# Early preparation of four head pairs and denser routing steps in a top-k attention and expert kernel

## The chip, the core and the metric

The kernel runs on one core of one Trainium2 chip. Five engines work from queues of their own: PE (matmuls and transposes), DVE (VectorE), ACT (ScalarE), POOL (GpSimd) and SP, which here issues nearly all DMAs. The metric is the device time of one execution in microseconds, median of several runs.

## The reference

Two layers are computed. The first is attention over q, k and v of 8 batches, 8 heads, 576 rows and 64 columns, in which each row keeps only its 32 largest scores. The second sends each of the 4608 output rows (512 wide) to one of 8 experts.

```
scores = (q @ k^T) / sqrt(64)
kth    = 32nd largest of each row
attn   = softmax over the scores >= kth
x      = attn @ v, heads side by side           # 4608 x 512
logits = x @ w_gate + modality_bias[modality]
e, p   = argmax and its softmax probability     # per row
out    = p * (relu(x @ w1[e]) @ w2[e])          # w1 512x1024, w2 1024x512
```

## The kernel before

Heads are taken in pairs, 32 pairs p from 0 to 31, four to a batch. A pair has 9 row tiles of 128 rows, so there are 288 tiles. One loop runs over steps i, with p = i // 9 and j = i % 9. A step works on several tiles at once: PE multiplies the scores of tile i+2 (L396), ACT copies them to SBUF (`Ssb`, L404), DVE takes the 8 largest of seven slices of tile i (seven MAX8, L411), merges those of tile i-1 (a chain of five, L422 to L424), ACT counts by a sign (`K`, L443) for tile i-3, POOL multiplies `y = Ssb * K` (L449) for tile i-4, DVE searches `y` of tile i-5 (L453), picks the threshold every third step (`eq`, `jk`, L460 to L462), ACT takes the exponential (`ex`, L467) of tile i-6, and DVE keeps the chosen ones of tile i-7 (`P`, L473). A one-element POOL instruction that reads `P` (`gate`, L477) holds POOL until that is done; `y` follows it.

Ahead of a pair its keys and queries must be turned and split. In steps j = 0, 1, 3 of pair p, `prep` turns tails, k and q of pair p+1 on PE; ACT writes a rounded part to the tile `st` (L275), PE subtracts it, and one step later ACT writes the rest (L279). Then `stack` issues DMAs that copy `st` to `ks` (six, L316) and `qs` (four, L318) in the layout of the matmul. There is one buffer for `st`.

When a batch's 36 steps are through, its 576 rows are routed: logits, argmax, ranks within experts (`route`), about 20 small DVE instructions, then five indirect DMAs from POOL (`send`, L620) that put the rows into lists per expert in DRAM (`xs`). Routing instructions lie in a queue `side`, slot choices in `rush`; each step takes up to SN = 4 of the one or RN = 6 of the other, and puts them among the seven MAX8 by holding up to four of these back (HOLD). For batches below EB = 3 (`early`) rows are turned in five steps running, and a send is issued behind `y`; for later ones the sends go through `side`, ahead of the step's gate and `y`.

Experts are worked in slots of 256 rows. `more_moe` starts a slot when its rows are counted (`seen`), and a budget (`spare_pe`, 3.3 a step less the listed costs) says how many matmuls of the slot a step takes. Twelve slots run inside the loop, in plain float32; those left run behind the loop in a three-term split form (`slot`). Until the first slot PE runs six filler matmuls a step (`keep_warm`, L931).

Of the kernel before, what the change touches and what calls it, by code (L numbers as in the profile page):

```python
# [9 lines left out]
FT = mybir.dt.float32  # L10
FR = mybir.dt.float32r
# [15 lines left out]
SN = 4  # L27
# [5 lines left out]
LJ = (5, 6)  # L33
# [2 lines left out]
QL = 2  # L36
HOLD = 4
NDIR = 2
KL = 2
LY = KL + 2  # L40
LT = LY + 1
# [9 lines left out]
PB = 6  # L51
COST = {"trans": 0.5, "qk": 0.5, "mix": 1.12, "rest": 0.22, "t": 0.11, "prep": 0.43, "logits": 1.2, "xrow": 0.54, "av": 0.42, "av8": 0.17}
RN = 6
QO = 0
EB = 3
RLF = (0, 1)
RXF = (3, 4, 5, 6, 7)
RLM = (3, 4)
# [12 lines left out]
def kernel(  # L71
# [43 lines left out]
    PAUSE = lambda: None  # L115
    WAIT = lambda: None

    def load(p, what, b=None, queues=(SP, SP, SP)):

        o = LD.setdefault(p, {})  # L120
        h0 = 2 * (p % HP)
        for nm in what:
            src = {"k": k, "q": q, "v": v}[nm]
            g = src[p // HP] if b is None else src[ds(b, 1)].rearrange("o h s d -> (o h) s d")
            if nm == "k":
                o["kq"] = ld.tile([128, 2, D], FT, name="kqt", bufs=1)
            t = vtb[p % 2] if nm == "v" else o["kq"][:64] if nm == "k" else o["kq"][64:]
            m = ld.tile([128, 2, 4, D] if nm == "v" else [128, 4, 2, D], FT, name=nm + "m", bufs=2 if nm == "v" else 1)
            if nm == "v":
                SP.dma_start(m.rearrange("p h c d -> p h (c d)"),  # L130
                             g[h0:h0 + 2, 0:512, :].rearrange("h (p c) d -> p h (c d)", c=4))
            else:
                for h in range(2):
                    queues[h].dma_start(m[:, :, h, :], g[h0 + h, 0:512, :].rearrange("(p c) d -> p c d", c=4))
            if nm == "v":
                tail = g[h0:h0 + 2, 512:, :].rearrange("h p d -> p h d")
                SP.dma_start(t[:64, 0:3:2, :], tail)
                SP.dma_start(t[64:, 1, :], g[h0 + 1, 512:, :])
            else:
                queues[2].dma_start(t, g[h0:h0 + 2, 512:, :].rearrange("h p d -> p h d"))  # L140
            o[nm] = (m, t)
# [78 lines left out]
    def reset_state():  # L220
        V.tensor_copy(base, eoff)
        V.tensor_copy(roff, eoff)
        V.tensor_copy(tokb, tokc)
# [42 lines left out]
        return load_mod(0, B)  # L266


    late, late_pe, later = [], [], []
    divide = deque()  # L270
    nxt = deque()

# [6 lines left out]
            A.activation(lo, ps, AF.Copy)  # L279
        late_pe.append(rest)  # L280

    def prep(p, part):


        d = PR.setdefault(p, {})
        if "st" not in d:
            d["st"] = wk.tile([128, 2, 2, S], FR, name="st", bufs=1)
        if part == "t":
            ps = psX.tile([128, 2, 64], FT, name="X")
            PE.matmul(ps.rearrange("p a b -> p (a b)"), LD[p]["kq"], idf, start=True, stop=False, is_transpose=True,  # L290
                      skip_group_check=True)
            split(*(d["st"][:, x, :, 512:] for x in range(2)), ps)
            return
        st = d["st"][:, :, "kq".index(part)]
        ps = psX.tile([128, 512], FT, name="X")
        for c in range(4):
            PE.matmul(ps[:, c * 128:(c + 1) * 128], LD[p][part][0][:, c], idf, start=(c == 0), stop=False,
                      is_transpose=True, skip_group_check=True)
        split(*(st[:, x, :512] for x in range(2)), ps)

        if part == "k":
            d["ks"] = wk.tile([128, 2, 2, S], FR, name="ks", bufs=2)
        else:
            d["qs"] = wk.tile([128, 2, S], FR, name="qs", bufs=2)
        for h in range(2):
            late_pe.append(lambda h=h: stack(p, part, h))

    def stack(p, part, h, queues=(SP, SP)):

# [20 lines left out]
    def first_pair():  # L330

        d = PR.setdefault(0, {})
        st = d["st"] = wk.tile([128, 2, 2, S], FR, name="st", bufs=1)
        (km, kt), (qm, qt) = LD[0]["k"], LD[0]["q"]
        pk, pa, pq = (psX.tile([128, 512], FT, name="X") for _ in range(3))

        def turn(ps, a, m, first=False, rows=slice(0, 128)):
            PE.matmul(ps[:, a:a + rows.stop - rows.start], m, idf[rows, rows], start=first, stop=False,
                      is_transpose=True, skip_group_check=True)

        def cut(which, a, b, ps):
            hi, lo = (st[:, x, which, a:b] for x in range(2))
            A.activation(hi, ps, AF.Copy)
            V.tensor_tensor(lo, ps, hi.bitcast(FT), op=OP.subtract)

# [12 lines left out]
        d["qs"] = wk.tile([128, 2, S], FR, name="qs", bufs=2)  # L358
        return lambda: cut(1, 128, S, pq[:, :S - 128])
# [233 lines left out]
    def route(lg, bias, oh, x5b, early=False):  # L593
# [24 lines left out]
        def send(c):  # L618
# [23 lines left out]
            lambda: V.tensor_reduce(sm, ez, axis=AX.X, op=OP.add),  # L642
            lambda: V.tensor_scalar(sm, sm, EPS, None, op0=OP.add),
            lambda: V.reciprocal(x5b[:, :, GW], sm),
            total,
            lambda: V.tensor_scalar(dest, ps5, float(ZROW), None, op0=OP.add),
            lambda: G.tensor_scalar(x5b[:, :, TOK], tokb, 1.0, 1.0, op0=OP.mult, op1=OP.mult),
# [226 lines left out]
    plan = {"ready": -1, "go": False}  # L874
    quiet = set()

    def more_moe():

        n = nslot[0]
        b = seen[0] // S  # L880
        full = 2 * b
        fits = lambda x: x >= PB
        if plan["ready"] == n:
            if moe or not plan["go"]:
                return
            chores()
            nslot[0] += 1
            nxt = full >= n + 2
            moe.extend(expert(n, True, nxt, fits(n + 1), True))
            if nxt:  # L890
                plan.update(ready=n + 1, go=True)
        elif full >= n + 1:
            now = SL[n - 1] if moe else {"xt": True, "used": [4, 4]}
            if not now["xt"]:
                return
            plan.update(ready=n, go=False)
            pick, rows, done, tok = sched(n, fits(n))
            free = []

            def begin():  # L900
                free.extend(now["used"])
                now["nxt"] = True

            def take(x, g):
                return lambda: (load_w1, load_w2)[x](n, g) if g < free[x] else None
            l1 = [lambda: [take(0, g)() for g in range(4)]]
            l2 = [take(1, g) for g in range(4)]
            go = [lambda: plan.update(go=True)]
            lead = l1 + [WAIT] + rows if sendq else rows + l1
            rush.extend(pick + [begin] + lead + done + [PAUSE] * (3 if b < 2 else 2) + tok + go)  # L910
            quiet.update(l2)
            side.extend([f for x in l2 for f in (x, PAUSE)])
# [152 lines left out]
    for i in range(LAST):  # L1065
# [40 lines left out]
        for f in lp:  # L1106
            f()
        cost += COST["rest"] * (len(lp) > 0)
        jj = FJ.get(j) if p == 0 else PREP.get(j)
        if p + 1 < NPAIR and jj:  # L1110
            prep(p + 1, jj)
            cost += COST["t" if jj == "t" else "prep"]
        if p + 2 < NPAIR and j in LJ:
            load(p + 2, "kq"[LJ.index(j)])
        if j == VJ and p < NPAIR:
            load(p, "v")
        b1, r = divmod(i - (TL + 2), 36)
# [32 lines left out]
        spare_pe = min(spare_pe + (STEP if i < NT + TL + END[0] else END[1]) - cost, CAP)  # L1150
        while seen[0] and spare_pe > 0:
            if i < NT + ME:
                more_moe()
            if not moe:
                break
            c, f, new = moe[0]
            if new and after:
                break
            moe.popleft()
            f()  # L1160
            spare_pe -= c
# [15 lines left out]
        for x, f in enumerate(lo):  # L1177
            b_.insert(LOP[x] if x < len(LOP) else len(b_), f)
        small_ = []
        for x in range(RN if rush else 0):  # L1180
            if rush and rush[0] is WAIT and sendq:
                break
            f = rush.popleft() if rush else PAUSE
            if f is PAUSE:
                break
            small_.append(f)
        if not small_:
            while bulk and not PJ[1] < j <= PJ[2]:
                chore.append(bulk.popleft())
            while chore:  # L1190
                small_.append(chore.popleft())
        for x in range(SN - len(small_)):
            if side and side[0] in quiet and PJ[1] < j <= PJ[2]:
                break
            f = side.popleft() if side and not rush else PAUSE
            if f is PAUSE:
                break
            small_.append(f)
# [130 lines left out]
    def slow():  # L1329
        Pb[:] = [wk.tile([128, 2 * S], FT, name=f"P{i}", bufs=1) for i in range(2)]  # L1330
        outs.clear()
        PR.clear()
        reset_state()
        for x in (scat, reads, fresh):
            x.clear()
# [71 lines left out]
```

## Time and profile before

| | |
|---|---|
| time, median of 3 | 1256.58 us (1254.93 to 1257.70) |
| profiled execution | 1256.33 us, span 1254.5 us |
| busy over the span | PE 94%, DVE 92%, ACT 81%, POOL 55% |
| mean granted TensorE clock | 0.983 |

The profile shows one execution. An engine's busy time is the union of its instructions; an instruction's own time can hold a wait inside. "Idle before" is the gap ahead of an instruction, with who ended it. The last six of the page's forty slices hold the slots behind the loop.

### The profile page before, as it was taken

To read this page: it belongs to the slowest core of one execution; us is meant where nothing else is said; L and a number is where in the kernel's file an instruction comes from. 1 tells how busy PE (TensorE), PEld (TensorE's weight loads), DVE (VectorE), ACT (ScalarE), POOL (GpSimd) and SP (SyncE) were. 2 spreads that over 40 slices of the span, in tenths; PEclk is the share of its full clock that TensorE was granted. 3 is DMA by queue.
4 is the path that set the end of the run, shared out by engine and by line. 5 is a ranking of instruction groups with operands and counts; after the bars stand their busy time and mean duration, and the time that the engine had idled before them with its cause. 6 is when DMAs were issued, how large, how long until landed. Compare 5 with 4: busy or idle time off the path is not lost. (4 is left out here: it accounts for less than half of the span.)

```text
span 1254.5 us, 29230 instructions
## 1 busy us (share of the span) xinstructions
PE 1182.1 (94%) x8141; PEld 929.6 (74%) x8141; DVE 1156.4 (92%) x5827; ACT 1018.0 (81%) x2042; POOL 687.8 (55%) x1342
## 2 busy tenths in 40 slices
PE   7888888899999999999999999999999999899995
PEld 6666676776868677786867777787868766799894
DVE  5999999999999999999999999999999995866764
ACT  4899988889989998988988988898889885555553
POOL 3555558456765576656865676556766772511110
PEclk8899998999999999999999999999999999999998
DMA  6665334775477557565476466666586423777563
GB/s 132 161 177 124 87 87 130 189 195 156 92 204 211 135 151 198 164 170 137 128 219 175 121 186 192 183 158 165 135 240 162 125 93 101 232 242 269 196 217 124
DMA packets 210133, 205.80 MB, mean 164 GB/s; under 512 B 106365, under 2 KB 155517, under 8 KB 209952
## 3 DMA queue, kind: packets, MB, share of 16 engines
q1 hardware_dynamic: 202384, 183.61, 54.1%
q0 software_dynamic: 6208, 19.54, 4.4%
q8 instruction: 70, 1.15, 0.4%
q14 instruction: 111, 0.91, 0.2%
q10 hardware_dynamic: 1360, 0.59, 0.2%
HBM read 123.35 MB, written 24.23 MB: 118 GB/s over the span
## 5 line engine op out<-in xcount | busy, mean ns | idle before, releaser
L411 DVE MAX8 cand<-Ssb 128x8 f32<-128x82 f32 (+1 forms) x2016 | 430.8, 231 | 8.9 <-ACT Ssb L404 8.9
L449 POOL TENSOR_TENSOR y<-Ssb,K 128x576 f32<-128x576 f32 x288 | 366.8, 1274 | 4.7 <-ACT K L443 4.1
L396 PE MATMUL S<-ks,qs 128*128 128x288 f32 x1016 | 232.9, 352 | 34.4 <-ACT Ssb L404 25.0
L404 ACT ACTIVATE Ssb<-S 128x576 f32<-128x576 f32 (+1 forms) x289 | 189.2, 655 | 72.0 <-PE S L396 53.0
L443 ACT ACTIVATE K<-Ssb,n 128x576 bf16<-128x576 f32 x288 | 227.8, 791 | 13.0 <-POOL y L449 12.5
L396 PEld LDWEIGHTS S<-ks,qs 128*128 128x128 f32 x1016 | 158.1, 193 | 91.9 <-issue 39.7
L467 ACT ACTIVATE ex<-Ssb,sm 128x576 f32<-128x576 f32 x288 | 226.1, 785 | 0.0
L453 DVE MAX8 mg<-y 128x8 f32<-128x576 f32 x288 | 214.6, 745 | 2.1 <-POOL y L449 2.1
L473 DVE SCALAR_TENSOR_TENSOR P<-Ssb,kth,ex 128x576 f32<-128x576 f32 x256 | 213.7, 835 | 0.6 <-PE T L488 0.3
L496 ACT ACTIVATE PT<-T 128x640 f32<-128x640 f32 (+1 forms) x288 | 191.5, 665 | 8.1 <-PE T L488 8.1
L803 PE MATMUL E<-xgT,w1b 128*128 128x256 f32 x768 | 188.3, 387 | 4.6 <-ACT xgT L784 2.4
L815 PE MATMUL E<-w2b,hT 128*128 128x512 f32 x384 | 182.7, 600 | 0.7 <-ACT hT L807 0.3
L488 PE MATMUL T<-idf,P 128*128 128x128 f32 x1152 | 170.1, 275 | 0.0
L803 PEld LDWEIGHTS E<-xgT,w1b 128*128 128x128 f32 x768 | 139.3, 191 | 31.1 <-ACT xgT L784 3.9
L477 POOL TENSOR_SCALAR spare<-P 1x1 f32<-1x1 f32 x256 | 47.8, 187 | 207.9 <-DVE mg L422 191.1
L516 PE MATMUL X<-PT,vm 128*64 128x256 f32 (+1 forms) x1536 | 147.8, 335 | 3.5 <-ACT st L279 2.5
L488 PEld LDWEIGHTS T<-idf,P 128*128 128x128 f32 x1152 | 136.5, 141 | 3.5 <-issue 1.3
L436 POOL TENSOR_SCALAR n<-mg 128x1 f32<-128x1 f32 x288 | 65.9, 229 | 109.1 <-DVE mg L424 100.8
L516 PEld LDWEIGHTS X<-PT,vm 128*64 128x64 f32 x1536 | 85.8, 137 | 50.4 <-issue 16.6
L815 PEld LDWEIGHTS E<-w2b,hT 128*128 128x128 f32 x384 | 66.5, 190 | 54.2 <-issue 50.5
L556 POOL TENSOR_TENSOR x<-x,rd 128x256 f32<-128x256 f32 (+1 forms) x80 | 53.8, 678 | 27.8 <-ACT x L560 27.8
L443 ACT ACTIVATION_READ_ACCUMULATOR K<-Ssb,n 128x1 f32 x288 | 61.5, 213 | 0.0
(208 smaller groups left out, 2248.7 us busy)
## 6 DMA issues: line engine op xcount, KB each, us to landing
w1b<-in_moe_w_dram SPq DMA_DIRECT2D x80, 512.0 KB, 5.6
w2b<-in_moe_w_dram SPq DMA_DIRECT2D x80, 512.0 KB, 5.6
ks<-st SPq DMA_DIRECT2D x64, 288.0 KB, 3.7
qs<-st SPq DMA_DIRECT2D x126, 144.0 KB, 2.9
ks<-st SPq DMA_DIRECT2D x62, 256.0 KB, 5.0
xg<-xs SPq DMA_DIRECT2D x20, 516.0 KB, 3.8
vm<-in_v_dram SPq DMA_DIRECT2D x32, 256.0 KB, 3.2
km<-in_k_dram SPq DMA_DIRECT2D x63, 128.0 KB, 4.1
```

The costliest lines, as they stand in the source:

```text
L396: PE.matmul(ps[:, hf, u - a:v - a], l, d["ks"][:, x, h, u + o:v + o], start=(n == 0), stop=(n == len(terms) - 1), skip_group_check=(j == 8))
L411: return [lambda s=s: V.max(c[:, s * 8:s * 8 + 8], T[i]["S"][:, bnd[s]:bnd[s + 1]]) for s in range(NSUB)]
L443: A.activation(t["K"], t["S"], AF.Sign, scale=2.0 ** -24 - 1.0, bias=t["n"][:, 1, i % 3:i % 3 + 1], accum_out=t["n"][:, 0, i % 3:i % 3 + 1])
L449: G.tensor_tensor(t["y"], t["S"], t["K"], op=OP.mult)
L453: V.max(t["mg"][:, i % 3, 24:32], t["y"])
L467: A.activation(t["ex"], t["S"], AF.Exp, bias=t["s"][:, i % 3:i % 3 + 1])
L473: V.scalar_tensor_tensor(t["P"], t["S"], kth[:, i:i + 1], t["ex"], op0=OP.is_ge, op1=OP.mult, accum_out=dn)
L488: PE.transpose(T[i]["pt"][:, x, :], (Pm if c == 4 else Pb[c % 2])[:, h * 512 + x * 128:h * 512 + x * 128 + 128], idf)
L496: A.activation(o, T[i]["pt"][:, :n], AF.Copy)
L516: PE.matmul(o.rearrange("p (a b) -> p a b", a=2) if j < 8 else o, l, r, start=(c == 0), stop=(c == 4), skip_group_check=True)
L803: PE.matmul(ps[:, f % 2], w1b[:, c, f * 128:(f + 1) * 128], xgT[:, c, :], start=(c == 0), stop=(c == KC - 1))
L815: PE.matmul(o["py"], hT[:, f, t * 128:(t + 1) * 128], w2b[:, f, :], start=(f == 0), stop=(f == FC - 1))
```

## The change

Four things change.

First, in steps of pairs 1 to 4 the kernel also loads k and q of pairs 8 to 11 into `w2b`, which no expert uses yet (steps j = 0 and 1, six DMAs), turns and splits them in steps j = 5, 6, 7 through the same `st`, and stores `st` in DRAM tiles `kept` (three DMAs a pair). For pairs 8 to 11 `prep` then does nothing but issue the ten stack DMAs from `kept`, and their loads are left out.

Second, EB becomes 4: the fourth batch is routed as the first three.

Third, while fewer than EB batches are counted, a step takes up to SF = 8 routing instructions, and up to RF = 9 slot choices before slot 6. For early batches a pause stands ahead of `total`.

Fourth, the planner counts no preparation cost for pairs 8 to 11, and starts no ready slot from step 288 on.

```diff
+AHEAD = dict(zip(range(1, 5), range(8, 12)))
+AJ = {5: "k", 6: "t", 7: "q"}
+SJ = {7: (slice(0, 1), slice(0, 512)), 8: (slice(0, 2), slice(512, None)), 9: (slice(1, 2), slice(0, 512))}
+SF, RF = 8, 9
-EB = 3
+EB = 4
...
+    def keep_st(f, w, c):
+
+        if f not in kept:
+            kept[f] = dr.tile([128, 2, 2, S], FR, name=f"kept{f}")
+        SP.dma_start(kept[f][:, :, w, c].bitcast(FT), stt[0][:, :, w, c].bitcast(FT))
...
-        if "st" not in d:
-            d["st"] = wk.tile([128, 2, 2, S], FR, name="st", bufs=1)
+        if p in kept:
+            if part != "t":
+                d["st"] = kept[p]
+                stacks(p, part, late_sp)
+            return
+        d["st"] = new_st()
...
             lambda: V.reciprocal(x5b[:, :, GW], sm),
+            *[PAUSE] * early,
             total,
...
-            if moe or not plan["go"]:
+            if moe or not plan["go"] or over:
...
+            cost += COST["t" if jj == "t" else "prep"] * (p + 1 not in kept)
             prep(p + 1, jj)
-            cost += COST["t" if jj == "t" else "prep"]
-        if p + 2 < NPAIR and j in LJ:
+        if p + 2 < NPAIR and j in LJ and p + 2 not in kept:
             load(p + 2, "kq"[LJ.index(j)])
+        if p in AHEAD:
+            if j < 2:
+                load(AHEAD[p], "kq"[j], bufs=abuf)
+            if j in AJ:
+                prep(AHEAD[p], AJ[j], True)
+        for x, (w, c) in SJ.items():
+            a_ = (i - x) // 9
+            if (i - x) % 9 == 0 and a_ in AHEAD:
+                keep_st(AHEAD[a_], w, c)
...
-                more_moe()
+                more_moe(i >= NT)
...
-        for x in range(RN if rush else 0):
+        for x in range((RN if nslot[0] >= PB else RF) if rush else 0):
...
-        for x in range(SN - len(small_)):
+        for x in range((SN if seen[0] >= EB * S else SF) - len(small_)):
```

Over the whole program DVE, ACT and POOL issue the same instructions in another order. PE issues 12 filler matmuls fewer, SP 12 DMAs more (the stores). From step 283 on, and behind the loop, the order of all engines is the same word for word apart from line numbers; 12 slots run in the loop as before.

On ACT, steps 23 and 24 (pair 2, j = 5 and 6; `K` is the sign count, `PT` the turned weights). Before:

```order
L404 ACTIVATE Ssb<-S 128x576
L496 ACTIVATE PT<-T 128x640
L443 ACTIVATE K,n<-Ssb,n 128x576
L467 ACTIVATE ex<-Ssb,sm 128x576
L404 ACTIVATE Ssb<-S 128x576
L496 ACTIVATE PT<-T 128x512
L443 ACTIVATE K,n<-Ssb,n 128x576
L467 ACTIVATE ex<-Ssb,sm 128x576
```

Now:

```order
L435 ACTIVATE Ssb<-S 128x576
L527 ACTIVATE PT<-T 128x640
L297 ACTIVATE st<-X 128x512
L474 ACTIVATE K,n<-Ssb,n 128x576
L498 ACTIVATE ex<-Ssb,sm 128x576
L435 ACTIVATE Ssb<-S 128x576
L527 ACTIVATE PT<-T 128x512
L301 ACTIVATE st<-X 128x512
L297 ACTIVATE st<-X 128x2x64
L474 ACTIVATE K,n<-Ssb,n 128x576
L498 ACTIVATE ex<-Ssb,sm 128x576
```

Three `st` writes have joined: the first part of k in one step, its rest and the first part of the tails in the next.

On DVE, the step of the first batch in which the slot choice begins (`tbl`, `s_key`, `s_oh`, `s_hit`, `s_sc` are its tables and picks). Before, step 56:

```order
L703 TENSOR_TENSOR tbl<-tbl 128x8
L713 SCALAR_TENSOR_TENSOR tbl<-tbl,eoff 128x8
L704 SCALAR_TENSOR_TENSOR s_key<-tbl,rev 128x8
L411 MAX cand<-Ssb 128x8
L714 TENSOR_TENSOR tbl<-tbl 128x8
L411 MAX cand<-Ssb 128x8
L705 MAX s_m_3585<-s_key 128x8
L411 MAX cand<-Ssb 128x8
L706 TENSOR_SCALAR s_oh<-s_key,s_m_3585 128x8
L411 MAX cand<-Ssb 128x8
L473 SCALAR_TENSOR_TENSOR P_153,den_162<-Ssb,kth,ex 128x576
```

Now, the beginning of step 54:

```order
L735 TENSOR_TENSOR tbl<-tbl 128x8
L745 SCALAR_TENSOR_TENSOR tbl<-tbl,eoff 128x8
L736 SCALAR_TENSOR_TENSOR s_key<-tbl,rev 128x8
L746 TENSOR_TENSOR tbl<-tbl 128x8
L737 MAX s_m_3579<-s_key 128x8
L738 TENSOR_SCALAR s_oh<-s_key,s_m_3579 128x8
L442 MAX cand<-Ssb 128x8
L732 TENSOR_TENSOR s_hit<-tbl,s_oh 128x40
L442 MAX cand<-Ssb 128x8
L733 TENSOR_REDUCE s_sc<-s_hit 128x5
L442 MAX cand<-Ssb 128x8
L749 TENSOR_SCALAR s_ft<-pos,s_sc 128x2
```

Nine choices stand in the step where six did, two steps earlier; six of them follow one another with no MAX8 between.

On POOL, the sends of the fourth batch (`x` by `rd` is the division of turned rows, `qbd` a copy of queries). Before:

```order
L477 TENSOR_SCALAR spare<-P_153 1x1
L449 TENSOR_TENSOR y<-Ssb,K 128x576
L556 TENSOR_TENSOR x_186<-x_186,rd 64x256
L436 TENSOR_SCALAR n<-mg 128x1
L620 DMA xs<-x_186,dest 38912x516
L533 MEMSET spare 1x1
L477 TENSOR_SCALAR spare<-P_154 1x1
L449 TENSOR_TENSOR y<-Ssb,K 128x576
L436 TENSOR_SCALAR n<-mg 128x1
L430 TENSOR_SCALAR sm<-mg 128x3
L620 DMA xs<-x_186,dest 38912x516
L533 MEMSET spare 1x1
```

Now:

```order
L508 TENSOR_SCALAR spare<-P_153 1x1
L480 TENSOR_TENSOR y<-Ssb,K 128x576
L587 TENSOR_TENSOR x_186<-x_186,rd 128x256
L587 TENSOR_TENSOR x_186<-x_186,rd 64x256
L651 DMA xs<-x_186,dest 38912x516
L564 MEMSET spare 1x1
L467 TENSOR_SCALAR n<-mg 128x1
L353 TENSOR_SCALAR qbd_145<-qs 128x64
L353 TENSOR_SCALAR qbd_146<-qs 128x64
L508 TENSOR_SCALAR spare<-P_153 1x1
L480 TENSOR_TENSOR y<-Ssb,K 128x576
L587 TENSOR_TENSOR x_186<-x_186,rd 64x256
```

The send stood ahead of a gate and its `y`; now it stands behind `y`, in the same step as two divisions and two copies.

## Rows read from the trace of the kernel before

**Rows 1.** Windows: length; busy us (count) of PE, PEld, DVE, ACT, POOL; clock; DMA

```profile
47.16:164.64 117.48, 100.54 (x841) 79.08 (x842) 117.48 (x649) 108.38 (x219) 64.16 (x128) 1.00 0.51 129
164.64:294.71 130.07, 118.28 (x854) 91.43 (x847) 128.11 (x703) 109.87 (x227) 79.49 (x154) 0.95 0.59 155
294.71:424.08 129.37, 127.34 (x873) 99.06 (x872) 128.65 (x704) 116.50 (x242) 81.44 (x158) 1.00 0.64 167
553.09:682.92 129.83, 127.44 (x860) 96.39 (x859) 129.14 (x694) 115.72 (x243) 85.35 (x162) 1.00 0.61 166
```

**Rows 2.** Groups by line, ACT: xcount | busy us, mean ns | idle before

```profile
L275 ACT ACTIVATE st<-X 128x512 fp32r<-128x512 f32 (+1 forms) x93 | 47.2, 508 | 1.4 <-PE X L290 1.3
...
L279 ACT ACTIVATE st<-X 128x512 fp32r<-128x512 f32 (+1 forms) x93 | 47.8, 514 | 0.0
...
L520 ACT ACTIVATE xT<-X 128x256 f32<-128x256 f32 (+1 forms) x96 | 32.0, 334 | 23.9 <-PE X L516 23.5
```

**Rows 3.** Timeline, ACT, 101 to 110 us: start, us, engine line op

```profile
101.49 0.28 ACT L275 ACTIVATE st<-X 128x128 fp32r<-128x128 f32 x1
101.70 0.78 ACT L443 ACTIVATE K<-Ssb,n 128x576 bf16<-128x576 f32 x1
...
106.83 0.65 ACT L404 ACTIVATE Ssb<-S 128x576 f32<-128x576 f32 x1 [0.18 <-DVE P L473]
...
107.85 0.61 ACT L279 ACTIVATE st<-X 128x512 fp32r<-128x512 f32 x1
108.35 0.78 ACT L443 ACTIVATE K<-Ssb,n 128x576 bf16<-128x576 f32 x1
...
109.97 0.65 ACT L404 ACTIVATE Ssb<-S 128x576 f32<-128x576 f32 x1
```

**Rows 4.** Timeline, SP: the six issues of a pair's key stacks

```profile
79.11 6.03 SPq L316 DMA_DIRECT2D ks<-st  x6
```

**Rows 5.** DMA issues, 50 to 165 us: median us to landing

```profile
ks<-st SPq DMA_DIRECT2D x8, 256.0 KB, 4.4
...
ks<-st SPq DMA_DIRECT2D x8, 32.0 KB, 4.3
```

**Rows 6.** Timeline, DVE, step 63: idle before it, who ended it

```profile
228.82 0.17 DVE L743 COPY sgt<-xg 128x2 f32<-128x2 f32 x1 [1.23 <-DMA xg<-xs]
```

**Rows 7.** Timeline, DVE and POOL: two plain cases, then instructions that waited

```profile
105.37 0.17 DVE L461 TENSOR_TENSOR jk<-eq,mg 128x27 f32<-128x27 f32 x1
...
109.07 0.80 DVE L473 SCALAR_TENSOR_TENSOR P<-Ssb,kth,ex 128x576 f32<-128x576 f32 x1
...
338.46 2.20 DVE L473 SCALAR_TENSOR_TENSOR P<-Ssb,kth,ex 128x576 f32<-128x576 f32 x1
...
599.85 1.93 DVE L473 SCALAR_TENSOR_TENSOR P<-Ssb,kth,ex 128x576 f32<-128x576 f32 x1
...
604.13 1.25 DVE L646 TENSOR_SCALAR dest<-r_ps 128x5 int32<-128x5 f32 x1
...
627.39 1.06 POOL L620 DMA_INDIRECT xs<-x,dest  x1 [0.16 <-issue]
...
628.87 1.27 POOL L449 TENSOR_TENSOR y<-Ssb,K 128x576 f32<-128x576 f32 x1
628.93 1.25 DVE L461 TENSOR_TENSOR jk<-eq,mg 128x27 f32<-128x27 f32 x1
```

**Rows 8.** Timeline, DVE: a plain step, then a routing step

```profile
100.00 0.22 DVE L422 MAX8 mg<-cand 128x8 f32<-128x56 f32 x1
100.13 0.23 DVE L411 MAX8 cand<-Ssb 128x8 f32<-128x82 f32 x1
...
100.28 0.08 DVE L422 MATCH_VALUE_LOAD cand<-mg,cand 128x8 f32 x1
...
200.19 0.21 DVE L422 MAX8 mg<-cand 128x8 f32<-128x56 f32 x1
200.43 0.09 DVE L422 MATCH_VALUE_LOAD cand<-mg,cand 128x8 f32 x1
```

More of the change, by code (lines that the diff above doesn't have):

```diff
@@ L116, with load @@
     WAIT = lambda: None
-    def load(p, what, b=None, queues=(SP, SP, SP)):
+    def load(p, what, b=None, queues=(SP, SP, SP), bufs=None):
         o = LD.setdefault(p, {})
@@ L125, in load @@
             if nm == "k":
-                o["kq"] = ld.tile([128, 2, D], FT, name="kqt", bufs=1)
+                o["kq"] = bufs["kq"] if bufs else ld.tile([128, 2, D], FT, name="kqt", bufs=1)
             t = vtb[p % 2] if nm == "v" else o["kq"][:64] if nm == "k" else o["kq"][64:]
-            m = ld.tile([128, 2, 4, D] if nm == "v" else [128, 4, 2, D], FT, name=nm + "m", bufs=2 if nm == "v" else 1)
+            m = bufs[nm] if bufs else ld.tile([128, 2, 4, D] if nm == "v" else [128, 4, 2, D], FT, name=nm + "m", bufs=2 if nm == "v" else 1)
             if nm == "v":
@@ L266, in routing_loads, with new_st @@
         return load_mod(0, B)
-    late, late_pe, later = [], [], []
+    kept = {}
+    aw = w2b.rearrange("p a b -> p (a b)")
+    abuf = {nm: aw[:, x * 512:x * 512 + 512].rearrange("p (c h d) -> p c h d", c=4, h=2) for x, nm in enumerate("kq")}
+    abuf["kq"] = aw[:, 1024:1152].rearrange("p (h d) -> p h d", h=2)
+    stt = []
+    def new_st():
+        if not stt:
+            stt.append(wk.tile([128, 2, 2, S], FR, name="st", bufs=1))
+        return stt[0]
+    def keep_st(f, w, c):
+        if f not in kept:
+            kept[f] = dr.tile([128, 2, 2, S], FR, name=f"kept{f}")
+        SP.dma_start(kept[f][:, :, w, c].bitcast(FT), stt[0][:, :, w, c].bitcast(FT))
+    late, late_pe, late_sp, later = [], [], [], []
     divide = deque()
@@ L280, in split, with prep @@
         late_pe.append(rest)
-    def prep(p, part):
+    def prep(p, part, early=False):
         d = PR.setdefault(p, {})
-        if "st" not in d:
-            d["st"] = wk.tile([128, 2, 2, S], FR, name="st", bufs=1)
+        if p in kept:
[4 more added lines that the diff above has]
+        d["st"] = new_st()
         if part == "t":
@@ L299, in prep, with stacks @@
         split(*(st[:, x, :512] for x in range(2)), ps)
+        if not early:
+            stacks(p, part, late_pe)
+    def stacks(p, part, late):
+        d = PR[p]
         if part == "k":
@@ L305, in prep @@
         for h in range(2):
-            late_pe.append(lambda h=h: stack(p, part, h))
+            late.append(lambda h=h: stack(p, part, h))
     def stack(p, part, h, queues=(SP, SP)):
@@ L332, in first_pair @@
         d = PR.setdefault(0, {})
-        st = d["st"] = wk.tile([128, 2, 2, S], FR, name="st", bufs=1)
+        st = d["st"] = new_st()
         (km, kt), (qm, qt) = LD[0]["k"], LD[0]["q"]
@@ L875, with more_moe @@
     quiet = set()
-    def more_moe():
+    def more_moe(over):
         n = nslot[0]
@@ L1108 @@
         cost += COST["rest"] * (len(lp) > 0)
+        while late_sp:
+            late_sp.pop(0)()
         jj = FJ.get(j) if p == 0 else PREP.get(j)
         if p + 1 < NPAIR and jj:
+            cost += COST["t" if jj == "t" else "prep"] * (p + 1 not in kept)
             prep(p + 1, jj)
-            cost += COST["t" if jj == "t" else "prep"]
-        if p + 2 < NPAIR and j in LJ:
+        if p + 2 < NPAIR and j in LJ and p + 2 not in kept:
             load(p + 2, "kq"[LJ.index(j)])
+        if p in AHEAD:
[7 more added lines that the diff above has]
+                keep_st(AHEAD[a_], w, c)
         if j == VJ and p < NPAIR:
@@ L1332, in slow @@
         PR.clear()
+        stt.clear()
         reset_state()
```

## The prediction

> **What bounds the kernel now.** Read the windows by stage first [rows 1]. Each covers 36 steps, that is four pairs. In the first (steps 11 to 46) there is no routing and no expert; the other three hold the routing of the first, second and fourth batch. In the first DVE is busy 117.48 of 117.48 us; in the others it lacks 1.96, 0.72 and 0.69 us. PE is also full from the third window line on (127.34 of 129.37), but how much it gets is set by the planner's budget, and DVE is as full beside it. The chain of waits covers only the last two microseconds and tells nothing. So inside the loop the time is DVE's work and what stretches it, while PE, ACT, POOL and the DMAs count only where they make DVE wait.
>
> The same rows give the size of what can be won. A step costs 117.48 / 36 = 3.26 us without routing. With it 36 steps take 129.37 to 130.07 us, so routing and slot choice cost 12 to 13 us a batch. The change issues the same DVE instructions in all, and nothing moves from step 283 on: the 12 slots in the loop and the slots behind it stay. No gain can come from the end; a loop that is shorter by so much ends the kernel earlier by as much. The profiled execution took 1256.33 us, 1.83 more than its span; that part stays.
>
> **The change part by part.**
>
> *Early preparation, pairs 1 to 4.* The cost falls on ACT: six writes a pair, 24 in all. Their mean is 0.508 and 0.514 us [rows 2], so 24 make 12.3 us. ACT is busy 108.38 us in that window [rows 1]; 108.38 + 12.3 = 120.7 is 3.2 over the window. That is the upper bound: an instruction's own time overlaps with the next one's. Counted from start to start, a long write takes 108.35 - 107.85 = 0.50 us and a short one 101.70 - 101.49 = 0.21; from `Ssb` to `Ssb` a step with one long write takes 109.97 - 106.83 = 3.14, so one without takes 2.64 [rows 3]. A pair then needs 9 x 2.64 + 8 x 0.50 + 4 x 0.21 + 3 copies `xT` of 0.33 [rows 2] = 29.6 us, against 117.48 / 4 = 29.4 that DVE needs. That is 0.2 a pair, 0.9 in four. The lower bound is 0, since ACT may lag two steps before DVE misses a tile. I take +0.9, the row that counts starts.
>
> PE gets 12 instructions more a pair in that window; it is free for 117.48 - 100.54 = 16.9 us there, 0.35 for each of the 48, and the fillers can slip. If that cover went, ACT would wait for the transposes and the bound of 3.2 would be the cost. Where the work is taken away (pairs 7 to 10, while they would have prepared 8 to 11) I count nothing: DVE is full in those windows, and an ACT or PE that is freer shortens no step. The planner spends PE's share on experts that are started only as rows are counted, so they too end in the same place.
>
> SP gets nine DMAs more a pair there, and the DMA engines are busy for 0.51 of that window [rows 1], so there is room. The new wait is on `st`: the early k is written three steps (9.8 us) after the stack of the regular k is begun, and that stack takes 6.03 us to issue [rows 4] and 4.4 us to land [rows 5], 10.4 together. ACT may thus wait 0.6 us a pair; behind it in ACT's queue stand the next tile's sign count and `Ssb`. Four times 0.6 is 2.4, inside the bound of 3.2.
>
> The Trainium skill (DMA: Bandwidth & Descriptors, section Specifications) says that pieces under 512 bytes go below line rate because they are read and rewritten, and the stored tails are in pieces of 256 bytes. The trace has such pieces too: the 32 KB stack of the tails landed in 4.3 us, no slower than the 256 KB one in 4.4 [rows 5]. By the rule the store of the tails would be the late one and the rival on landings below likelier; by the row it costs nothing, and I go by the row.
>
> *Fuller slot choice.* With nine choices a step, by the order, the load of the first slot's w1 is issued in step 55 instead of 58, while its rows are fetched in step 58 instead of 60: three steps ahead instead of two. DVE's wait for these rows was 1.23 us, one of few real gaps [rows 6]. I take -1.2; the other end is 0, if the rows themselves and not the weights ahead of them were slow.
>
> *The fourth batch routed early.* Three stretched instructions stand there now [rows 7]. `P` took 1.93 us at 599.85 where a plain one takes 0.80, `dest` 1.25, and `jk` 1.25 at 628.93 where a plain one takes 0.17. The last shows why: POOL issued a send at 627.39 for 1.06 us, so its `y` ran late, from 628.87 to 630.14, and `jk`, which lay on top of it, ended at 630.18. With sends behind `y` this order does not arise. The three stretches are 1.1 each, 3.3 together. But the batches that are routed early have such a case too: `P` took 2.20 us at 338.46 in the second, 1.4 too much. So 1.9 is left; I take -1.9, with 0 and -3.3 as ends.
>
> The Trainium skill (SBUF — State Buffer, section Who interferes with whom) says that a VectorE instruction with two SBUF inputs and a GpSimd instruction that reads SBUF shut each other out for the whole instruction, and that issue order decides who waits. `jk` agrees, ending 0.04 us after `y`. By that rule the crowded POOL step shown in the order makes new waits; that is the first rival.
>
> *Denser routing steps.* In the order the steps that carry such instructions fall from 16 to 14, 16 to 14, 17 to 14 and 14 to 12 in the first four batches, nine fewer. In a routing step MAX8s are held back, and the chain's first MAX8 is followed at once by the load of its values: 0.24 us from 200.19 to 200.43. In a plain step a MAX8 of 0.15 us fits in between and the same way takes 0.28 [rows 8]. So 0.24 - 0.13 = 0.11 us is lost a step, 1.0 us in nine. Against it, six of nine choices follow each other with nothing between, and each depends on one before. That has no row. I bound it by the same 0.11 us of exposed latency, for some ten instructions in each of the three dense steps, +3.3, so that the sum of this part can be +2.3; on the other side, a step less may also spare one stretch of 1.1 in two of the batches, -3.2. I take -1.0.
>
> Sum: +0.9 - 1.2 - 1.9 - 1.0 = -3.2, against the profiled 1256.33 that is 1253.1. The median of the runs is 0.25 higher, so I forecast 1253.
>
> **The rivals.**
>
> *The waits come back, no change.* In the new order a POOL step holds `y`, two divisions, a send and two copies. POOL then runs over the step and the next `y` lies on `eq`, `jk` or `P`, at 1.1 to 1.4 us a time [rows 7]. Two more such waits over four batches, 2.2 to 2.8 us, make 1253.1 + 2.8 = 1256. For it: 338.46 shows it in an early batch. Against it: the load per batch is the same, only two steps shorter.
>
> *Landings, slower.* If the added loads and stores make the stack land 2 us later, 6.4 instead of 4.4, then ACT waits 10.4 + 2 - 9.8 = 2.6 us a pair before the early k. It has no time to catch up (29.6 of 29.4), so 10.4 us in four pairs reach DVE. With the 4.1 gained elsewhere that is 1256.3 + 10.4 - 4.1 = 1262.6. It decides from a landing of about 5.2 us on, where the waits eat 4.1. For it: the issue and landing already fill the three steps. Against it: DMA is busy half the time.
>
> *All good ends.* 0 - 1.2 - 3.3 - 3.2 = -7.7: 1248.6. For it: ACT's lag of two steps; against it: that each part would have to end well.
>
> **How the numbers follow.** I give the forecast 0.42, the waits that come back 0.32, the landings 0.14, the good ends 0.12. A measurement of this kernel cannot tell a change under 0.2%, 2.5 us, from none. The forecast lies just outside, so a little of its chance falls within: faster 0.52, same 0.34, slower 0.14. The range for 8 in 10 leaves out most of the landings and the edge of the good ends: 1248 to 1259.
>
> **What would show it.** In the profile after, the window of pairs 1 to 4 should stay at 117 to 121 us for 36 steps, with ACT near full; a wait of ACT's `st` on a DMA, or DVE waiting for `Ssb`, would speak for the landings. DVE's wait of 1.23 us before `sgt` should go. In the fourth batch no `dest` or `jk` of 1.25 us should be left, and its 36 steps should take about 128 us. The first three batches should take about 0.3 us less each; if `P`, `eq` or `jk` reach 1.2 us or more there oftener than now, the waits have come back. The forecast is wrong if the 36-step windows from 164 us on, taken together, do not shorten, or if the part behind step 283 changes its length.

## The result, and the profile after

The changed kernel is slower. Its median is 1262.19 us against 1256.53 us of the kernel before (six runs each), a ratio of 1.0053 with a 95% interval of 1.004 to 1.0067. The forecast was 1253. The profiled execution took 1262.47 us, its span is 1260.7.

The windows by stage answer to [rows 1]. They are again bounded by the starts of the `P` that close steps 10, 46, 82, 118, then 154, 190, and last 226, 262, 283. Columns: length; busy us (count) of PE, PEld, DVE, ACT, POOL; clock; DMA share; GB/s.

```profile
46.38:163.87 117.49, 107.16 (x889) 84.97 (x890) 117.49 (x649) 114.64 (x243) 64.17 (x128) 1.00 0.70 184
163.87:294.96 131.09, 117.76 (x835) 90.40 (x828) 130.37 (x704) 106.37 (x213) 80.48 (x156) 0.95 0.58 159
294.96:428.85 133.89, 128.76 (x852) 98.24 (x851) 130.32 (x704) 113.96 (x234) 80.86 (x158) 0.99 0.54 145
558.59:687.90 129.31, 123.83 (x843) 93.71 (x842) 128.36 (x692) 114.59 (x237) 82.92 (x162) 1.00 0.62 167
816.61:945.44 128.83, 127.44 (x851) 96.44 (x850) 128.21 (x688) 112.28 (x234) 84.52 (x163) 1.00 0.63 172
945.44:1024.34 78.90, 76.13 (x523) 57.70 (x521) 76.88 (x402) 70.86 (x148) 54.58 (x101) 1.00 0.54 146
```

The first stage is what it was: 117.49 for 117.48 us, although ACT is now busy for 114.64 us of it and the DMA engines for 0.70. The loss lies elsewhere. Stage by stage, the changed kernel less the one before: first batch +1.0, second +4.5, third +0.7, fourth -0.5, fifth -1.6, sixth -2.4, steps 263 to 283 +4.4. That is 6.1 us, the difference of the spans (6.2). Behind step 283 both take 235.6 to 236.4 us.

**The second batch: rows that come late.** DVE, the gate copies of the first and of the third slot (start, us, engine, line, operation; in brackets idle time before it and who ended it):

```profile
221.87 0.15 DVE L775 COPY sgt<-xg 128x2 f32<-128x2 f32 x1
...
365.31 0.17 DVE L775 COPY sgt<-xg 128x2 f32<-128x2 f32 x1 [2.26 <-DMA xg<-xs]
```

The wait of [rows 6] is gone in the first batch and a longer one has come in the second. SP's queue ahead of it, after:

```profile
357.36 1.41 SPq L787 DMA_DIRECT2D w2b<-in_moe_w_dram  x2
359.63 0.35 SPq L764 DMA_DIRECT2D xg<-xs  x1
```

and before:

```profile
352.43 2.15 SPq L751 DMA_DIRECT2D w1b<-in_moe_w_dram  x4
362.89 0.34 SPq L732 DMA_DIRECT2D xg<-xs  x1
```

POOL issued the last send of this batch at 352.05 now and at 357.13 before. Before, SP waited 7.5 us for that send to land and issued the load of the rows 5.8 us behind the send's issue. Now the load came 7.6 us behind it, with weights of the running slot ahead of it in SP's queue, and the rows took up to 5.7 us more. `sgt` stands three steps behind the last send in both.

**`dest` under POOL's divisions.** DVE after, the `dest` of the first four batches:

```profile
189.69 1.23 DVE L678 TENSOR_SCALAR dest<-r_ps 128x5 int32<-128x5 f32 x1
...
334.54 1.78 DVE L678 TENSOR_SCALAR dest<-r_ps 128x5 int32<-128x5 f32 x1
...
468.00 1.79 DVE L678 TENSOR_SCALAR dest<-r_ps 128x5 int32<-128x5 f32 x1
...
598.22 2.47 DVE L678 TENSOR_SCALAR dest<-r_ps 128x5 int32<-128x5 f32 x1
```

Before, the first three (the fourth, 1.25, stands in [rows 7]):

```profile
194.43 0.56 DVE L646 TENSOR_SCALAR dest<-r_ps 128x5 int32<-128x5 f32 x1
...
337.86 0.15 DVE L646 TENSOR_SCALAR dest<-r_ps 128x5 int32<-128x5 f32 x1
...
468.98 0.17 DVE L646 TENSOR_SCALAR dest<-r_ps 128x5 int32<-128x5 f32 x1
```

Together 7.27 us now and 2.13 before. POOL after, beside the one at 334.54:

```profile
333.88 1.27 POOL L480 TENSOR_TENSOR y<-Ssb,K 128x576 f32<-128x576 f32 x1
335.12 1.18 POOL L587 TENSOR_TENSOR x<-x,rd 128x256 f32<-128x256 f32 x2
336.60 1.07 POOL L651 DMA_INDIRECT xs<-x,dest  x1 [0.31 <-DVE dest L678]
```

`dest` began inside `y` and ended at 336.32, when `y` and both divisions behind it were through (336.30). The stretches of [rows 7] in the fourth batch did go, as forecast: `P` takes 0.80 at 601.27 and `jk` 0.16 at 616.22. They gave back 2.2 us, and `dest`, 2.47 for 1.25, took 1.2 of it.

**The end of the loop.** The changed kernel has a wait for PE there that the one before lacks, and `P` behind `y` in four steps running (279 to 282, 1.23 to 1.47 us). DVE, then POOL, after:

```profile
973.20 0.29 DVE L618 TENSOR_TENSOR lt<-X,rd 128x128 f32<-128x128 f32 x1 [1.52 <-PE X L610]
...
1016.56 1.38 DVE L504 SCALAR_TENSOR_TENSOR P<-Ssb,kth,ex 128x576 f32<-128x576 f32 x1
```

```profile
1016.05 1.28 POOL L480 TENSOR_TENSOR y<-Ssb,K 128x576 f32<-128x576 f32 x1
```

The same step before has `P` first and `y` long after it:

```profile
1012.13 0.80 DVE L473 SCALAR_TENSOR_TENSOR P<-Ssb,kth,ex 128x576 f32<-128x576 f32 x1
```

```profile
1014.17 1.27 POOL L449 TENSOR_TENSOR y<-Ssb,K 128x576 f32<-128x576 f32 x1
```

### The profile page after: what moved, and what is told of

It is laid out like the page before. It is cut to its first block, busy times and chain, and to the rows that moved or that the text cites. A ratio compares the mean times of both kernels' runs of the same rounds, so it can differ in the third digit from the quotient of the medians.

```text
span 1260.7 us, 29251 instructions
## 1 busy us (share of the span) xinstructions
PE 1186.6 (94%) x8129; PEld 931.0 (74%) x8129; DVE 1160.3 (92%) x5827; ACT 1016.5 (81%) x2042; POOL 687.4 (55%) x1342
## 5 line engine op out<-in xcount | busy, mean ns | idle before, releaser
L435 ACT ACTIVATE Ssb<-S 128x576 f32<-128x576 f32 (+1 forms) x289 | 188.5, 653 | 74.5 <-PE S L427 51.0
L453 DVE MAX8 mg<-cand 128x8 f32<-128x56 f32 x288 | 61.4, 213 | 0.2
```

## The experiments

Four theories were tried. A: the fuller steps cost the time, through `dest` and `sgt`. B: the early preparation costs it, through its transfers or through the share of PE that it frees. C: the end of the loop has two patterns, by the steps in which the planner starts the last slots, and the changed kernel fell into the dearer one. D: routing the fourth batch early costs a wait of its own on POOL. A stage whose code is the same in two kernels differed by up to 0.9 us between their profiles (the kernel before, and the first of the two planner runs below, up to step 205), so a smaller difference of a stage says nothing. The 108 steps from 47, taken together, differ so by 1.3 us (388.5 and 387.2), and by 1.2 us between the changed kernel and the second planner run (394.7 and 395.9).

The parts first. In all of these runs the new code stays, and constants switch it; the pause ahead of `total` goes with the fuller steps. The planner's rule for step 288 was not switched by itself.

```diff
 early preparation alone
-SF, RF = 8, 9
+SF, RF = 4, 6
-EB = 4
+EB = 3
-            *[PAUSE] * early,
```

> The early preparation alone (EB = 3, four routing instructions and six choices a step as before, no pause ahead of total). Theory A, the fuller steps cost the time: nothing is paid in the first stage (its 36 steps took 117.49 us in the changed kernel, 117.48 before), so this is within 2 us of before, ratio 0.9985 to 1.0015. Theory B, the stored preparation costs it, through its transfers and through the share of PE that it frees for experts: 3 to 6 us slower, ratio 1.0025 to 1.005.

```diff
 fuller steps alone
-AHEAD = dict(zip(range(1, 5), range(8, 12)))
+AHEAD = {}
-EB = 4
+EB = 3
```

> The fuller steps alone (SF = 8, RF = 9, the pause ahead of total; no early preparation, EB = 3). Theory A: dest, the first table instruction and eq lie on POOL's y and two divisions in each of the first three batches (2 to 3 us more stretched time in all), and the gate copy sgt meets rows that are not there yet (up to 2.3 us): 3 to 6 us slower, ratio 1.0025 to 1.005. Theory B: within 1.5 us of before.

```diff
 fourth batch early, alone
-AHEAD = dict(zip(range(1, 5), range(8, 12)))
+AHEAD = {}
-SF, RF = 8, 9
+SF, RF = 4, 6
-            *[PAUSE] * early,
```

> The fourth batch routed early, alone (four routing instructions and six choices a step, no pause, no early preparation). Both theories: the three stretches of 1.1 us that the fourth batch had go, and one such comes back: 0 to 2 us faster, ratio 0.9985 to 1.0. If sends behind y make DVE wait as much as sends ahead of it did, no change.

```diff
 the changed kernel without the fuller steps
-SF, RF = 8, 9
+SF, RF = 4, 6
-            *[PAUSE] * early,
```

> The changed kernel without the fuller steps (early preparation and EB = 4 kept, four routing instructions and six choices a step, no pause). Theory A: 0 to 2 us faster than before, ratio 0.998 to 1.001, so 5 to 8 us faster than the changed kernel. Theory B: still 3 to 6 us slower than before, ratio 1.0025 to 1.005.

Then what these left open: the planner's two patterns, forced by one unit each way, `dest` put later in its step, and POOL's gate copy put later.

```diff
 the kernel before, late pattern (the early one in the changed kernel: i == 205, += 1.0)
+        if i == 206:
+            spare_pe -= 1.0
         while seen[0] and spare_pe > 0:
```

> The kernel before, with one unit taken once from the planner's share of PE at step 206: slots 1 to 9 start in the same steps, the last three start at steps 244, 262 and 282 instead of 242, 260 and 281, as in the changed kernel. Theory C, the end of the loop has two patterns, and the changed kernel fell into the dearer: steps 227 to 262 take 128.5 to 128.8 us instead of 131.2, steps 263 to 283 take 78.8 instead of 74.5, all else as before, so 2 us slower, ratio 1.001 to 1.0025. Rival: what these steps cost in the changed kernel comes from work that was put off upstream, and this run stays within 0.7 us of before.

> The changed kernel, with one unit added once to the planner's share of PE at step 205: the last three slots in the loop start at steps 242, 260 and 281, as before. Theory C: steps 263 to 283 take 74.5 us instead of 78.9 and steps 227 to 262 some 2 us more, so about 2 us less than the changed kernel (1260 for its 1262.2), ratio to before 1.0025 to 1.0045: two thirds of the loss stay, in the first three batches. Rival: no change against the changed kernel.

```diff
 the changed kernel, the pause moved
+            *[PAUSE] * early,
             lambda: V.tensor_reduce(sm, ez, axis=AX.X, op=OP.add),
             lambda: V.tensor_scalar(sm, sm, EPS, None, op0=OP.add),
             lambda: V.reciprocal(x5b[:, :, GW], sm),
-            *[PAUSE] * early,
             total,
```

> The changed kernel with the pause put ahead of the three instructions r_sm, r_sm, reciprocal instead of behind them, so that they stand ahead of total and dest in the same step and dest comes some 0.5 us later; by the planner the last three slots then start at 242, 260 and 281. Theory A: dest no longer meets POOL's two divisions at their start; its time in the first three batches falls from 1.8 us to under 1.0, their 108 steps take 391 to 393 us instead of 394.7, and with the 2 us of the other pattern at the end the whole is 1257 to 1259. Rival: whatever stands there is shut out (r_sm instead of dest), the 108 steps stay at 394.7, and the whole is 1260.

```diff
 the changed kernel without the fuller steps, gate copy later
-... [PAUSE] * (3 if b < 2 else 2) + tok ...
+... [PAUSE] * (3 if b < 2 else 6 if b == EB else 2) + tok ...
```

> Early preparation and EB = 4 without the fuller steps, as in the run without them, but four more pauses ahead of POOL's gate copy sgt of the slots that follow the fourth batch. There POOL waited 10.9 us for the rows and DVE 8.6 us for y behind it. Theory D, that wait alone is the price of EB = 4: steps 155 to 190 take 128 to 129 us instead of 137.2, and the whole is 1251 to 1254, faster than before, ratio 0.9965 to 0.999. Rival: the rows are late for PE too, the slot starts as late as they land, and the wait turns up elsewhere: not faster than before.

Last, the two halves of the fuller steps, the wait of the second batch, and the early preparation without the late pattern.

```diff
 the changed kernel, one more pause ahead of sgt
-... [PAUSE] * (3 if b < 2 else 2) + tok ...
+... [PAUSE] * (3 if b < 3 else 2) + tok ...
```

> The changed kernel with one more pause (three instead of two) ahead of the gate copy sgt of the slots that follow the second batch. There DVE waited 2.26 us for the rows in step 100. Theory A: that wait goes, the 36 steps from 83 take 131 to 132 us instead of 133.9, and the whole is 2 us less than the changed kernel: 1260. Rival: the rows are late for PE as well and the time stays, 1262.

```diff
 routing instructions only                 choices only (and no pause ahead of total)
-SF, RF = 8, 9                            -SF, RF = 8, 9
+SF, RF = 8, 6                            +SF, RF = 4, 9
```

> The changed kernel with eight routing instructions a step and the pause, but six slot choices (SF = 8, RF = 6). Theory A, the routing part puts dest under POOL's two divisions: dest takes 1.2 to 2.5 us in each of the first four batches as in the changed kernel, the 108 steps from 47 take 391 to 394 us (387.5 without either of the two). Rival, the choices do it: dest under 0.6 in three of four, 388. The slots' starts fall into a third pattern by the planner (the last at 241, 259 and 278), so the whole says less: 1256 to 1262.

> The changed kernel with four routing instructions and no pause, but nine slot choices a step (SF = 4, RF = 9). Theory A: dest as before (under 0.6 us in the first three batches); what nine choices cost is sgt, which comes one step nearer to its rows: 0 to 3 us in the first three batches, their 108 steps 388 to 390. The wait of POOL's sgt behind the fourth batch, 8.6 us for DVE without the fuller steps, stays at 4 to 9, so the whole is 1258 to 1264. Rival: the 108 steps take 394 as in the changed kernel.

```diff
 early preparation alone, early pattern
+        if i == 205:
+            spare_pe += 1.0
         while seen[0] and spare_pe > 0:
```

> The early preparation alone, with one unit added once to the planner's share of PE at step 205, so that the last three slots start at 242, 260 and 281 as before. Theory C: the 2 us that the early preparation alone cost were the other pattern at the end and no more, so this is the time of before: ratio 0.999 to 1.001. Rival: the transfers of the stored preparation cost something in the middle too, ratio 1.0015 to 1.003.

What was measured. The ratio is to the kernel before on the same chip; the stages are the lengths from the profile, in us, between the starts of the `P` that close them.

| kernel | ratio (95% interval) | steps 47-82 | 83-118 | 119-154 | 155-190 | 191-226 | 227-262 | 263-283 |
|---|---|---|---|---|---|---|---|---|
| before | 1 | 130.1 | 129.4 | 129.0 | 129.8 | 130.3 | 131.2 | 74.5 |
| changed | 1.0053 (1.0040-1.0067) | 131.1 | 133.9 | 129.7 | 129.3 | 128.7 | 128.8 | 78.9 |
| early preparation alone | 1.0021 (1.0006-1.0037) | 129.0 | 130.7 | 128.5 | 130.5 | 129.7 | 128.5 | 80.0 |
| the same, early pattern | 1.0001 (0.9989-1.0013) | 128.7 | 130.2 | 128.5 | 130.4 | 129.5 | 130.8 | 74.5 |
| fuller steps alone | 1.0056 (1.0034-1.0077) | 130.6 | 132.1 | 133.6 | 128.8 | 129.3 | 128.6 | 78.9 |
| fourth batch early, alone | 1.0059 (1.0038-1.0080) | 130.4 | 129.0 | 129.1 | 135.5 | 131.7 | 128.8 | 78.8 |
| without fuller steps | 1.0058 (1.0037-1.0078) | 128.8 | 130.6 | 128.5 | 137.2 | 131.4 | 130.2 | 74.5 |
| the same, gate copy later | 1.0007 (0.9996-1.0019) | 128.9 | 130.2 | 128.5 | 130.4 | 131.9 | 130.3 | 74.5 |
| before, late pattern | 1.0021 (1.0008-1.0034) | 129.7 | 128.5 | 129.0 | 129.0 | 130.4 | 128.8 | 78.4 |
| changed, early pattern | 1.0037 (1.0023-1.0051) | 131.6 | 134.0 | 130.3 | 129.4 | 128.7 | 131.3 | 74.5 |
| changed, pause moved | 1.0049 (1.0034-1.0065) | 134.0 | 131.1 | 131.1 | 129.2 | 130.4 | 130.4 | 74.5 |
| changed, pause ahead of `sgt` | 1.0045 (1.0031-1.0060) | 130.8 | 130.1 | 131.5 | 129.6 | 128.7 | 128.8 | 78.9 |
| routing instructions only | 1.0088 (1.0070-1.0107) | 135.2 | 131.6 | 130.1 | 129.9 | 129.5 | 130.1 | 79.5 |
| choices only | 1.0075 (1.0061-1.0090) | 131.7 | 131.3 | 128.8 | 136.9 | 131.4 | 130.2 | 74.5 |

*The two patterns.* The last column has two values, 74.5 and 78.4 to 80.0, with the stage before it at 130.2 to 131.3 or 128.5 to 128.8 (the routing-only kernel is a third case). The kernel before with one unit of budget taken away at step 206 is alike up to there and ends in the late pattern (windows as above):

```profile
809.33:938.12 128.79, 127.40 (x851) 96.38 (x850) 128.17 (x689) 112.25 (x234) 83.94 (x163) 1.00 0.64 172
938.12:1016.56 78.44, 75.66 (x520) 57.62 (x520) 77.82 (x401) 70.45 (x148) 53.12 (x101) 1.00 0.54 148
```

and the changed kernel with one unit added ends in the early one:

```profile
818.62:949.91 131.29, 130.72 (x883) 100.30 (x882) 129.78 (x692) 118.33 (x246) 85.35 (x164) 1.00 0.63 172
949.91:1024.41 74.50, 71.68 (x497) 54.28 (x495) 74.16 (x398) 67.00 (x139) 52.56 (x99) 1.00 0.55 150
```

By the medians the first costs 1257.37 - 1254.72 = 2.7 us, and the second gains about 2 (1260.26 for 1262.19, ratio 1.0037 for 1.0053). The last two intervals overlap, but the stages from step 227 on fall from 207.7 to 205.8 us. Theory C holds in both directions, near the 2 us expected. What fills these steps differs (the wait of `lt` for PE is 1.5 us in the changed kernel and 0.2 in the first of the two), their length hardly. Which slots start when comes from a budget in which early preparation and denser steps book other costs, though the work is the same.

*Early preparation.* Alone it missed both expectations: between them, at 1.0021. All of that goes with the late pattern: with the early one it is at 1.0001, as expected. So theory B falls as to the transfers, and the share of PE that is freed counts only through the pattern. The store does show, as a wait of ACT in the changed kernel (ACT's groups by line in the first stage, idle before at the end of the row; then the longer of the two waits on ACT and the store on SP that it waited for):

```profile
L297 ACT ACTIVATE st<-X 128x512 fp32r<-128x512 f32 (+1 forms) x24 | 12.2, 509 | 1.3 <-DMA kept<-st 1.3
...
72.29 0.28 ACT L297 ACTIVATE st<-X 128x128 fp32r<-128x128 f32 x1 [0.96 <-DMA kept<-st]
...
68.65 0.54 SPq L289 DMA_DIRECT2D kept<-st  x1
```

Both waits are of the next pair's tails for the store of the tails before them, the pieces of 256 bytes; it had landed some 3.6 us after its issue in the one case and 3.2 in the other. ACT waited 1.3 us in all, and DVE's stage is as long as before. With the early preparation and without the fuller steps the wait for the first slot's rows is gone too. But it is also gone with the fuller steps alone. The windows of the early preparation alone in the early pattern, first stage and first two batches:

```profile
45.08:162.58 117.50, 106.97 (x888) 84.78 (x889) 117.50 (x650) 114.97 (x243) 64.23 (x128) 1.00 0.70 184
162.58:291.26 128.68, 114.30 (x838) 89.00 (x831) 127.95 (x703) 106.25 (x214) 79.17 (x154) 0.97 0.54 148
291.26:421.44 130.18, 125.52 (x853) 96.32 (x851) 129.49 (x704) 112.60 (x231) 80.17 (x158) 1.00 0.60 157
```

*The fourth batch early.* Both theories missed: alone it is at 1.0059 where 0.9985 to 1.0 was expected. The changed kernel without the fuller steps, at 1.0058, lies above the range of theory B, and not in B's place: the cost is in the fourth batch's stage again. Without the fuller steps the first slot that follows that batch has its gate copy on POOL before its rows have come. POOL, in the changed kernel without the fuller steps:

```profile
636.72 0.19 POOL L771 TENSOR_SCALAR sgt<-xg 128x2 f32<-128x2 f32 x1 [10.92 <-DMA xg<-xs]
```

SP in the same run, which issued the rows behind four loads of weights and a pair's stack:

```profile
611.88 10.73 SPq L782 DMA_DIRECT2D w1b<-in_moe_w_dram  x4
625.66 5.66 SPq L347 DMA_DIRECT2D ks<-st  x6
632.78 0.36 SPq L763 DMA_DIRECT2D xg<-xs  x1
```

and DVE, which searches the `y` that stood behind it on POOL:

```profile
638.47 0.76 DVE L484 MAX8 mg<-y 128x8 f32<-128x576 f32 x1 [8.61 <-POOL y L480]
```

With four more pauses that wait is gone, the stage falls from 137.2 to 130.4, and the whole from 1.0058 to 1.0007. Theory D is right on the wait. That the kernel would then be faster than before was wrong: the stage ends 0.6 above the one before, and the next 1.6. In the changed kernel the fuller steps bring these rows earlier (`xg` issued at 620.71), POOL waits 1.0 us, and the stage is 0.5 shorter than before. So the changed kernel as a whole is no faster without the fuller steps (1.0058 for 1.0053): what its first three batches give back goes into this wait.

*The fuller steps.* Alone they cost as much as the whole change, 1.0056, a little over the range of theory A. In the changed kernel the 108 steps from 47 take 394.7 us, and 387.9 without the fuller steps: 6.8 us. Beside the kernel before, the fuller steps alone make them 396.3 for 388.5: 7.8 us. But the instructions that pay are not the same in both. With the fuller steps alone no DVE instruction waits for `xg`, and in the third batch, 4.6 us longer than before, `dest` takes 0.17. There `P` and `eq` are stretched (`P` began inside `y` and ended behind two divisions):

```profile
468.37 2.77 DVE L504 SCALAR_TENSOR_TENSOR P<-Ssb,kth,ex 128x576 f32<-128x576 f32 x1
...
473.10 1.34 DVE L491 TENSOR_TENSOR eq<-i9s,n 128x27 f32<-128x27 f32 x1
```

The halves, the first of them with the pause ahead of `total`, split as expected as to `dest`, not in size. Instructions of its line (count: least, median, most ns, first and last start), routing only:

```profile
L678 DVE TENSOR_SCALAR dest<-r_ps x8: 153/894/1794, 188.4 to 1082.2; 128x5 int32<-128x5 f32 x8
```

choices only:

```profile
L677 DVE TENSOR_SCALAR dest<-r_ps x8: 148/166/802, 193.5 to 1084.8; 128x5 int32<-128x5 f32 x8
```

Eight routing instructions a step put `dest` under the divisions (1.09 to 1.79 us in the first four batches). But the 108 steps take 396.9 with them (391 to 394 expected), the whole is 1264.91 (1262 at most expected), and the first slot's rows were met too early again:

```profile
224.91 0.17 DVE L775 COPY sgt<-xg 128x2 f32<-128x2 f32 x1 [5.07 <-DMA xg<-xs]
```

Nine choices alone take 391.8 (388 to 390 expected), without any wait of DVE for `xg`; 2.9 of the 3.9 over 387.9 is in the first batch, with a wait of 1.3 us for `Ssb` that no theory had. The halves do not add up: 9.0 and 3.9 us alone, 6.8 together. The wait on POOL behind the fourth batch stays there, as expected (136.9 in its stage), and the whole is 1264.95, a microsecond over the range.

Moving the pause missed: 1262.23, no gain, although the last slots start in the early pattern. The 108 steps take 396.2 (391 to 393 expected). DVE in that run:

```profile
188.68 1.24 DVE L675 TENSOR_SCALAR r_sm<-r_sm 128x5 f32<-128x5 f32 x1
...
190.24 0.17 DVE L678 TENSOR_SCALAR dest<-r_ps 128x5 int32<-128x5 f32 x1
...
226.84 0.17 DVE L775 COPY sgt<-xg 128x2 f32<-128x2 f32 x1 [2.59 <-DMA xg<-xs]
...
336.56 2.44 DVE L678 TENSOR_SCALAR dest<-r_ps 128x5 int32<-128x5 f32 x1
```

In the first batch `r_sm` is shut out in its stead, in the second `dest` meets `y` at its very start, and a wait for rows comes in the first batch. That is its rival, and dearer than the rival said (394.7 and 1260).

One more pause ahead of `sgt` took the wait of 2.26 us away, and the second batch falls from 133.9 to 130.1. The third rises by 1.8, although `dest` takes 0.17 in it: now others are stretched there, `P` and `s_ft`, which take 0.80 and 0.27 when they are free.

```profile
465.82 1.62 DVE L504 SCALAR_TENSOR_TENSOR P<-Ssb,kth,ex 128x576 f32<-128x576 f32 x1
...
471.01 1.60 DVE L749 TENSOR_SCALAR s_ft<-pos,s_sc 128x2 f32<-128x2 f32 x1
```

The whole fell by 1.0 us, half of what was expected; the intervals (1.0045 for 1.0053) overlap.

No version beats the kernel before. The nearest is the early preparation alone in the early pattern, at the same time.

## Why the prediction was wrong

The step that failed is the pair of terms for the denser steps: "fuller slot choice", -1.2, and "denser routing steps", -1.0. Together they were to take 2.2 us off; the denser steps cost the first three batches 6.8 us. I had priced their latency, and the saving of a stretch. What they do is move instructions against two clocks that do not move with them: POOL's divisions and the landing of the rows. In the changed kernel `dest` grew by 4.80 - 0.88 = 3.9 us in these batches, and `sgt` waited 2.3; that is 6.2 of the 6.8. This is read from one profile, in which other instructions grew and shrank beside them. That the denser steps cost the time is shown by the runs with and without them. Which instruction pays changes with the order: `dest` and `sgt` here, `P` and `eq` with the fuller steps alone, `P` and `s_ft` when `sgt` was freed. No run took all of them away at once.

Term by term:

- Early preparation, +0.9: measured 0. ACT's lag took it all, the waits of 1.3 us for the store included. They were not the wait that I priced, of the early k for the stack of the regular k, which did not come. For the store of the tails I had gone by a row of the stack, which stays inside SBUF; the store itself landed in 3.2 and 3.6 us where ACT waited for it. The rival on landings gave 1262.6, which is near the measured time by chance: no part of the loss is in the first stage. Its limit of 5.2 us was also wrong by its own working: 4 x (6.03 + L - 9.8) reaches 4.1 at a landing L of 4.8.
- The wait at `sgt`, -1.2: it went in the first batch, and a longer one came in the second. The early preparation alone ends it, and so do the fuller steps alone, so the changed kernel does not tell which did, and why either does (the loads of pair 8 that are left out stand in these steps) was not tried. I had looked at one place, and at the load of the rows instead of at the copy, which stands a few steps behind the last send (three in the second batch) whether the rows have landed or not.
- The fourth batch, -1.9: the stretches of `P` and `jk` went as forecast, `dest` took 2.47 instead of 1.25, and the stage gained 0.5. That the early route alone would make the stage 5.7 us longer, by a POOL instruction that waits 7.6 us for a DMA ahead of `y`, I did not see. Its rows stood in SP's queue behind three loads of weights and a stack.
- The first rival, waits that come back under the crowded POOL step, was the right mechanism with the wrong size and the wrong instruction. It allowed two waits of 1.1 to 1.4 us, on `P`, `eq` or `jk`, and 1256; there are four on `dest` alone, up to 2.47, for it can be kept out over three POOL instructions in a row. `P`, `eq` and `jk` reach 1.2 us once in the first three batches, as often as before.
- "The planner spends PE's share on experts that are started only as rows are counted, so they too end in the same place" was the step that cost +2.0. They end in the same place from step 283 on, where I compared the order, but between steps 227 and 282 they lie otherwise, and `P` and `y` lock in another order there.
- The fifth batch gained 1.6 us in the changed kernel. None of the runs isolates that; it is open.

The sum is now: 394.7 - 387.9 = +6.8 for the fuller steps, 387.9 - 388.5 = -0.6 for the rest of the change in the first three batches (inside the spread), -0.5, -1.6, and +2.0 for the pattern, together +6.1.

## What to carry to other kernels

Here a denser schedule on the full engine lost more to neighbours with clocks of their own than its latency was worth. So ask of each instruction that moves what the neighbour is doing at the new time, and how long the data it reads have been on their way. Where a planner books costs, compare the order over the whole loop, not at its end alone: one unit of budget moved three slots by one or two steps and cost 2 us with the same work. And test parts of a change alone and together: here three parts that each cost 0.2 to 0.6% alone cost 0.5% in all.

## What the runs showed of the hardware

A short DVE instruction that meets POOL's work can be kept out over several POOL instructions that follow each other without a gap: `dest`, 0.15 to 0.17 us when it is free, took 1.78 us over `y` and two divisions, and 2.44 when it began with `y`. But it is not always kept out so long. In the changed kernel a short instruction got in between two such divisions (POOL, then DVE):

```profile
594.31 1.19 POOL L587 TENSOR_TENSOR x<-x,rd 128x256 f32<-128x256 f32 x2
...
594.48 0.47 DVE L674 TENSOR_SCALAR r_sm<-r_sm 128x5 f32<-128x5 f32 x1
```

It ended at 594.95, and the divisions at 595.50. With the routing instructions only, the `dest` of the fifth batch ended at 741.30 behind `y` alone, while the division after it ran from 741.23 to 741.84. What decides between the two was not found.

`dest` has a single input in SBUF, as has `r_sm` (1.24 us in the run with the pause moved). The Trainium skill (SBUF — State Buffer, section Who interferes with whom) names such a tensor_scalar among the operations that can take the port that GpSimd uses. These rows agree with it; the rule on two inputs, by which I chose what to look at, was too narrow.
